# A spectral mixer and token MLP on one core: the filter rows in 20 loads of two pieces instead of 28 of three

## The chip, the cores and the metric

The kernel runs on one core of a Trainium2 chip. The metric is the device time of one execution in microseconds (us); lower is better. The core has engines that run side by side, each through its own list of instructions: TensorE (PE, matrix products; its weight loads are shown as PEld), VectorE (DVE), ScalarE (ACT), GpSimd (POOL) and SyncE (SP), which here only issues transfers. Transfers (DMA) between the device memory and the on-chip memory run on 16 DMA engines beside the compute engines. An engine goes through its list in order, and where an instruction needs what another engine or a transfer makes, it waits on a semaphore; all that stands behind it on the same engine waits too.

## What is computed

The input is a sequence of 2048 rows with 512 numbers each. It is normalised row by row, transformed by a real two-dimensional FFT, multiplied by a complex filter `w_r + 1j * w_i` of 2048 x 257 numbers, transformed back and added to the input. A second part normalises the sum, and mixes along the sequence with an MLP of 1376 hidden units:

```
h  = x + irfft2(rfft2(layernorm(x)) * (w_r + 1j * w_i))
u  = gelu(einsum("bsd,sf->bdf", layernorm(layernorm(h)), w1) + b1)
h2 = h + (einsum("bdf,fs->bds", u, w2) + b2) transposed
```

The second line's two normalisations are the one ahead of the MLP part and the one inside it. All inputs and outputs are in bf16.

## The kernel before

The transforms are matrix products with constant tables. The 2048 rows are held as 128 partitions x 16 (`NS2`), and the transforms go through these stages, named after the helper functions that emit them:

- A (line 593): the first step of the transform along the sequence, 16 groups of four matmuls, with the tables F scaled by each row's deviation into FS. Y holds the result.
- B (line 637), the transform along the 512 columns, and C (line 652), the second step along the sequence, for 16 chunks c of 8 of the 128 columns of Y. B is evicted into six buffers Bsb, C into two buffers Xsb, each for a pair of chunks.
- P (`emit_P`, line 669; the instruction is on line 674): VectorE multiplies one chunk by the filter. P of chunk c reads `W[:, 2*c:2*c+2]`, that is two of the 32 filter rows (`NTAU`) that each partition holds, both components, and writes one of six buffers P.
- I (`emit_I`, instruction on line 692): the first inverse step, eight matmuls for a chunk, which read P. Its eviction Ie (lines 708 and 709) goes to TT.
- Bi, Ai (lines 771, 801 to 808 and the variants for the first group): the remaining inverse steps, then the sum h, its normalisation HH, and the MLP: `m1` (line 844, first weights W1), the gelu, and `m2` (line 962, second weights W2), with the output added and stored.

The filter tile W has 128 partitions x 32 rows x 2 components x 256 columns in bf16, 4 MB. The filter rows lie in device memory in another order than the partitions want, and half of them are read backwards, so W can't be loaded in one transfer. The list `pieces` on line 510 cuts the 32 rows of all partitions into stretches. For each stretch, each component and each of two groups of partitions there is one load of the stretch read forward and one read backward; the stretch that starts at row 0 needs one more load for its first row. Each load writes 32 partitions in runs of 512 bytes. That gives 12 loads for the first stretch and 8 for each other.

All loads of one stretch form a group (`group=f"W{pi}"`) with one semaphore. In `gen_sync` an instruction that reads anything of a group waits for the count of the whole group:

```
v = count[d.lane] if d.is_dma else d.lane_idx
```

So a P waits until every load of the stretch that holds its two rows has landed. P0 to P3 read the stretch of rows 0 to 7, P4 to P8 that of rows 8 to 17, P9 to P15 that of rows 18 to 31.

The order of the work on each engine is fixed. `schedule` (line 249) takes written lists for the compute engines (line 979), which name nearly every operation of these stages. On VectorE the products and the evictions between them stand there as `P0 P1 Ie0_0 P3 P2 Be7 P4 Be8 P5 Ie2_0 P7 P6 Ie4_0 P9 P8 Ie6_0 P10 P11 Ie7_0 P13 P12 Ie10_0 P14 P15`. On TensorE the same stretch ends with `C10p I6 I5 B14 C12p I7 B15 I8 I9 C14 I10 C15 I11 I12 I13 I14 I15`. SP issues transfers by their `prio`: first X and F (a part of X is issued by ScalarE), then E, Lm and Hm, then the filter loads stretch by stretch, then ID, GD and IF, the eight loads of W1 and the eleven of W2. Those behind the filter loads also wait for the last eviction of stage A (`gate`, line 737). GpSimd issues three small loads, of the biases B1s and B2s.

Of the kernel before, what the change touches and what calls it, by code (L numbers as in the profile page):

```python
# [465 lines left out]
def build_kernel(nc, A_x, A_w_r, A_w_i, B_w1, B_b1, B_w2, B_b2, out, verbose=False):  # L466
# [40 lines left out]
    dma("ld_L", "sp", Lm[:], cin["L"][:, :, :, :], 2 << 16, prio=0.51)  # L507
    dma("ld_H", "sp", Hm[:], cin["H"][:, :, :, :], 1 << 17, prio=0.52)

    pieces = [(0, 8), (8, 18), (18, 32)]  # L510
    for pi, (ta, tb) in enumerate(pieces):
        for comp, wsrc in enumerate((A_w_r, A_w_i)):
            wv = wsrc.rearrange("(q r) k -> q r k", r=64)
# [515 lines left out]
def bass_sequential_preLN__spectral_gfnet__mixer_token_mlp__prompt_kernel(  # L1029
    nc,  # L1030
    A_x,
    A_w_r,
    A_w_i,
    B_x,
    B_w1,
    B_b1,
    B_w2,
    B_b2,
    out,
):  # L1040
    build_kernel(nc, A_x, A_w_r, A_w_i, B_w1, B_b1, B_w2, B_b2, out)
# [28 lines left out]
```

## Time and profile before

| what | value |
|---|---|
| median of 5 runs | 130.63 us (129.92 to 132.82) |
| the profiled execution | 130.18 us, of which the profile's span is 128.4 us |
| TensorE busy | 121.7 us, 95% of the span |
| VectorE busy, ScalarE busy | 65.1 us each, 51% |
| filter products on VectorE (line 674) | 16 of 0.68 us, from 20.2 to 36.3 us |
| filter loads issued by SP | 28, from 6.53 to 25.94 us |
| granted TensorE clock | 1.0 throughout |

The profile shows one execution. Times in it count from the start of its span. A line of a timeline gives start, duration, engine, source line, operation, what it writes and reads, and how many instructions are merged; a bracket at its end tells how long the engine had been idle before and what ended the wait. A line of a DMA view gives the tile and its source, the issuing queue, the number of issues, the size of one and the median time from issue to landing. A line of windows gives, for a stretch of time, each engine's busy time and instruction count, the granted TensorE clock, the mean busy share of the DMA engines and the rate in GB/s. Matmuls overlap, so that the durations of single ones add up to more than the time they take together.

### The profile page before, as it was taken

The page shows a single profiled execution, that of the slowest core. Times are in us where ns is not written, and L with a number is a line of the kernel's source. Part 1 is how long each engine was busy: PE and PEld are TensorE (multiplying, and loading weights), DVE is VectorE, ACT ScalarE, POOL GpSimd, SP SyncE. Part 2 cuts the span into 40 slices and gives each one's busy share as a digit, 9 for nine tenths or more (in the row PEclk, how much of TensorE's full clock was granted, in tenths as well). Part 3 has the DMA queues.
Part 4 walks back from the last instruction along what each step waited for, and adds up shares of the span by engine and source line. Part 5 has one row for each costly group of instructions (what it writes and reads, how often), then busy time and mean ns, then how long its engine had stood idle before and what let it go on. Part 6 is the DMA issues. An engine that isn't in the chain of part 4 may idle for free.

```text
span 128.4 us, 2036 instructions
## 1 busy us (share of the span) xinstructions
PE 121.7 (95%) x777; PEld 74.4 (58%) x786; DVE 65.1 (51%) x141; ACT 65.1 (51%) x137; POOL 12.6 (10%) x33
## 2 busy tenths in 40 slices
PE   6969979999999999999999999999999999999990
PEld 2337657777776655545444444456666666666660
DVE  1679948997978999967750000000423323324322
ACT  4779979999968989898777711222000000000000
POOL 0049980310000000000000000000000000000000
PEclk9999999999999999999999999999999999999999
DMA  3999899999999999999100000000111121121121
GB/s 107 339 396 371 254 209 212 300 278 357 394 422 422 420 417 417 276 361 400 59 0 0 0 0 5 0 0 0 41 67 55 41 79 49 41 82 41 41 84 41
DMA packets 16505, 22.71 MB, mean 177 GB/s; under 512 B 1552, under 2 KB 12304, under 8 KB 16368
## 3 DMA queue, kind: packets, MB, share of 16 engines
q1 hardware_dynamic: 15808, 21.66, 49.1%
q10 hardware_dynamic: 576, 0.92, 2.0%
q8 instruction: 6, 0.10, 0.3%
q0 software_dynamic: 112, 0.01, 0.2%
q14 instruction: 3, 0.02, 0.1%
HBM read 20.49 MB, written 2.10 MB: 176 GB/s over the span
## 4 chain that ended last, share of the span: by engine, by line
PE 86%; DMA 6%; SPq 2%; ACT 1%; issue 1%; DVE 1%; POOL 0%
PE ps L844 29%; PE ps L962 28%; PE ps L692 6%; DMA F<-c_F 6%; PE ps L637 6%; PE ps L771 5%; PE ps L652 3%; SPq L490 2%; PE ps L593 2%; PE ps L808 2%; PE ps L968 2%; ACT Y L607 1%; PE ps L911 1%; DVE OUT L974 1%; POOL FS L577 0%
## 5 line engine op out<-in xcount | busy, mean ns | idle before, releaser
L844 PE MATMUL ps<-HH,W 128*128 128x512 bf16 (+1 forms) x168 | 39.4, 379 | 0.2
L962 PE MATMUL ps<-GT,W 128*128 128x512 bf16 (+1 forms) x162 | 35.7, 379 | 0.2
L974 DVE SCALAR_TENSOR_TENSOR OUT<-ps,B2f,H 128x512 bf16<-128x512 f32 x16 | 12.0, 751 | 46.7 <-PE ps L962 24.4
L962 PEld LDWEIGHTS ps<-GT,W 128*128 128x128 bf16 (+1 forms) x165 | 23.7, 144 | 12.0
L844 PEld LDWEIGHTS ps<-HH,W 128*128 128x128 bf16 (+1 forms) x170 | 16.9, 100 | 17.6 <-issue 0.2
L944 ACT ACTIVATE GT<-ps,B1f 128x512 bf16<-128x512 f32 (+1 forms) x11 | 7.0, 691 | 12.7 <-PE ps L844 11.8
L818 DVE TENSOR_TENSOR H<-ps,X 128x512 bf16<-128x512 f32 x14 | 9.7, 691 | 4.0 <-PE ps L808 3.4
L824 ACT ACTIVATE SQ<-H,nm 128x512 bf16<-128x512 bf16 x14 | 10.1, 721 | 2.7 <-DVE H L818 2.4
L674 DVE TENSOR_TENSOR P<-Xsb,W 128x1024 bf16<-128x1024 bf16 x16 | 10.4, 684 | 0.9 <-DMA W<-in_A_w_i_dram 0.8
L559 DVE BATCH_NORM_STATS2 st<-X 128x6 f32<-128x512 bf16 x13 | 8.3, 679 | 3.7 <-DMA X<-in_A_x_dram 3.7
L781 ACT ACTIVATE EO<-ps 128x512 bf16<-128x512 f32 x15 | 8.8, 587 | 0.9 <-PE ps L771 0.7
L637 PE MATMUL ps<-E,Y 128*128 128x256 bf16 x64 | 8.5, 273 | 0.7 <-ACT Y L607 0.7
L593 PE MATMUL ps<-FS,X 128*128 128x256 bf16 x64 | 7.9, 273 | 1.3 <-POOL FS L577 1.2
L771 PE MATMUL ps<-GD,TT 128*128 128x256 bf16 x60 | 9.0, 272 | 0.1
L692 PE MATMUL ps<-Hm,P 128*128 128x128 bf16 x128 | 8.9, 220 | 0.0
L692 PEld LDWEIGHTS ps<-Hm,P 128*128 128x128 bf16 x128 | 7.4, 98 | 1.7 <-issue 1.3
L577 POOL TENSOR_SCALAR FS<-F,rs 128x256 bf16<-128x256 bf16 x16 | 7.4, 481 | 7.8 <-DMA F<-c_F 7.2
L533 PE MATMUL ps<-WM 128*128 128x512 bf16 (+1 forms) x19 | 7.0, 523 | 1.2 <-DVE eps L525 1.2
L665 ACT ACTIVATE Xsb<-ps 128x1024 bf16<-128x1024 f32 (+1 forms) x9 | 8.0, 884 | 0.0
L641 ACT ACTIVATE Bsb<-ps 128x512 bf16<-128x512 f32 x13 | 7.3, 594 | 1.2 <-PE ps L637 1.2
L593 PEld LDWEIGHTS ps<-FS,X 128*128 128x128 bf16 x64 | 5.4, 97 | 3.7 <-POOL FS L577 2.2
L771 PEld LDWEIGHTS ps<-GD,TT 128*128 128x128 bf16 x60 | 5.8, 98 | 3.0 <-ACT EO L781 0.2
(70 smaller groups left out, 97.2 us busy)
## 6 DMA issues: line engine op xcount, KB each, us to landing
W<-in_B_w_dram SPq DMA_DIRECT2D x8, 688.0 KB, 13.5
W<-in_B_w_dram SPq DMA_DIRECT2D x10, 512.0 KB, 18.3
out_dram<-OUT SPq DMA_DIRECT2D x16, 128.0 KB, 1.7
X<-in_A_x_dram SPq DMA_DIRECT2D x4, 256.0 KB, 6.7
F<-c_F SPq DMA_DIRECT2D x4, 256.0 KB, 7.0
IF<-c_IF SPq DMA_DIRECT2D x1, 1024.0 KB, 8.0
W<-in_A_w_r_dram SPq DMA_DIRECT2D x4, 224.0 KB, 3.8
W<-in_A_w_i_dram SPq DMA_DIRECT2D x4, 224.0 KB, 4.3
```

Of the source, the lines that this page charges most:

```text
L559: K.op(f"bn{n2}", "dve", lambda e, eng, n2=n2: eng.bn_stats(st[:, n2, 0:6], X[:, n2, :]), ins=[X[:, n2, :]], outs=[st[:, n2, 0:6]], occ=62 ...
L593: r = eng.matmul(ps[:, b, 256 * u:256 * u + 256].rearrange("p (a b) -> p a b", a=2), X[:, n2, 128 * t:128 * t + 128], fr if t < 2 else fa, ...
L637: r = eng.matmul(o, Y[:, k, c, :], E[:, k, :].rearrange("p (h r) -> p h r", h=2), start=(i == 0), stop=(i == 3), skip_group_check=True)
L674: return eng.tensor_tensor(P[:, :, :, :], x.unsqueeze(2).broadcast_to([NP, 2, 2, 256]), W[:, 2 * c:2 * c + 2, :, :], ALU.mult)
L692: r = eng.matmul(o, P[:, h, m, par::2], Hm[:, v, m, :].rearrange("p (m r) -> p m r", r=4), start=(h == 0 and m == 0 and (par == 0 or b != ...
L771: r = eng.matmul(o, TT[:, q, n2, par, :], GD[:, par, q, :], start=(i == 0), stop=(i == 3), skip_group_check=True)
L781: return eng.activation(eo[:, :], ps[:, bE, :], ACT.Copy)
L818: K.op(f"h{n2}", "dve", lambda e, eng: eng.tensor_tensor(H[:, n2, :], ps[:, bA, :], X[:, n2, :], ALU.add), ins=[ps[:, bA, :], X[:, n2, :]] ...
L824: K.op(f"sq{n2}", "act", lambda e, eng: eng.activation(sq[:, :], hsrc, ACT.Square, bias=nm[:, n2, 0:1], accum_out=s2t[:, n2, 0:1]), ins=[h ...
L844: return eng.matmul(ps[0:Mt, bank, :], W1[:, n2, 128 * t:128 * t + Mt], HH[:, n2, :], start=(n2 == 0), stop=(n2 == 15), skip_group_check=True)
L962: r = eng.matmul(ps[:, b, :], W2[t][0:Kt, n2::16], GT[0:Kt, t, :], start=(t == 0), stop=(t == NFT - 1), skip_group_check=True)
L974: K.op(f"fin{n2}", "dve", lambda e, eng, n2=n2, b=b: eng.scalar_tensor_tensor(OUT[:, n2, :], ps[:, b, :], B2f[:, n2:n2 + 1], H[:, n2, :], ...
```

## The change

The 32 rows are cut into two stretches, rows 0 to 11 and rows 12 to 31, instead of three.

```
-    pieces = [(0, 8), (8, 18), (18, 32)]
+    pieces = [(0, 12), (12, 32)]
     for pi, (ta, tb) in enumerate(pieces):
         for comp, wsrc in enumerate((A_w_r, A_w_i)):
             wv = wsrc.rearrange("(q r) k -> q r k", r=64)
```

There are 12 loads for the first stretch (four each of 192, 16 and 176 KB) and 8 of 320 KB for the second; before there were 12 (128, 16 and 112 KB), 8 of 160 KB and 8 of 224 KB. The bytes are the same. P0 to P5 now wait for the first group and P6 to P15 for the second. In VectorE's order the first product that needs the second group is P7; before, P4 and P9 were the first of their groups. The instructions of TensorE, VectorE, ScalarE and GpSimd and their order stay as they are; the list of SP is shorter by eight, and what stands behind the filter loads moves forward by that much.

More of the change, by code (lines that the diff above doesn't have):

```diff
@@ L508, in build_kernel @@
     dma("ld_H", "sp", Hm[:], cin["H"][:, :, :, :], 1 << 17, prio=0.52)
-    pieces = [(0, 8), (8, 18), (18, 32)]
+    pieces = [(0, 12), (12, 32)]
     for pi, (ta, tb) in enumerate(pieces):
```

## The prediction

> **What bounds the kernel now.** I read the page's busy table and chain first, for the engine that sets the end.
>
> ```profile
> PE 121.7 (95%) x777; PEld 74.4 (58%) x786; DVE 65.1 (51%) x141; ACT 65.1 (51%) x137; POOL 12.6 (10%) x33
> ...
> PE 86%; DMA 6%; SPq 2%; ACT 1%; issue 1%; DVE 1%; POOL 0%
> ```
>
> The reader is to see that TensorE is the bound and that its own waits are short. A filter load can move the end only through VectorE: load, product P (L674), the inverse matmuls (L692) that read P, and TensorE's place in its fixed order. So the second view is the groups, for a P that waits on a load.
>
> ```profile
> L674 DVE TENSOR_TENSOR P<-Xsb,W 128x1024 bf16<-128x1024 bf16 x16 | 10.4, 684 | 0.9 <-DMA W<-in_A_w_i_dram 0.8
> ```
>
> One wait, 0.8 us. The third view, VectorE's timeline from 23.7 to 37 us, says which P it is. In VectorE's written order the products stand P0 P1 P3 P2 P4 P5 P7 P6 P9 P8 P10 and so on, with evictions (CAST) in between.
>
> ```profile
> 24.41 0.69 DVE L674 TENSOR_TENSOR P<-Xsb,W 128x1024 bf16<-128x1024 bf16 x1
> 25.02 0.68 DVE L642 CAST Bsb<-ps 128x512 bf16<-128x512 f32 x1
> 25.62 0.68 DVE L674 TENSOR_TENSOR P<-Xsb,W 128x1024 bf16<-128x1024 bf16 x1
> 26.22 0.68 DVE L709 CAST TT<-ps 128x512 bf16<-128x512 f32 x1
> 26.82 1.28 DVE L674 TENSOR_TENSOR P<-Xsb,W 128x1024 bf16<-128x1024 bf16 x2
> 28.12 0.69 DVE L709 CAST TT<-ps 128x512 bf16<-128x512 f32 x1
> 29.62 1.29 DVE L674 TENSOR_TENSOR P<-Xsb,W 128x1024 bf16<-128x1024 bf16 x2 [0.80 <-DMA W<-in_A_w_i_dram]
> ...
> 35.03 1.28 DVE L674 TENSOR_TENSOR P<-Xsb,W 128x1024 bf16<-128x1024 bf16 x2
> ```
>
> P7 and P6 are the pair at 26.82, P9 and P8 the pair at 29.62: P9 waits for the third piece. From 29.62 VectorE runs without a break to the end of P15 at 36.31. The fourth view is the DMA issues, each of the last loads of the three pieces asked for alone (issued at 13.93, 19.20 and 25.27).
>
> ```profile
> W<-in_A_w_i_dram SPq DMA_DIRECT2D x1, 112.0 KB, 3.0
> ...
> W<-in_A_w_i_dram SPq DMA_DIRECT2D x1, 160.0 KB, 5.1
> ...
> W<-in_A_w_i_dram SPq DMA_DIRECT2D x1, 224.0 KB, 4.3
> ```
>
> So the pieces are complete at 16.9, 24.3 and 29.6 us. The first products that need them start at 20.20, 24.41 and 29.62. The last view is the TensorE timeline at the end of this stage.
>
> ```profile
> 32.30 1.06 PE L692 MATMUL ps<-Hm,P 128*128 128x128 bf16 x16
> ...
> 34.50 2.57 PE L692 MATMUL ps<-Hm,P 128*128 128x128 bf16 x40
> ```
>
> The 16 take 1.06 us. Without the last one's own 0.22 that is 15 steps of 0.056. The 40 at this step would take 39 x 0.056 + 0.22 = 2.40, and they take 2.57. The 0.16 that is left is the last group, I15, waiting for P15. This is all that TensorE loses here to a late VectorE.
>
> **The change, part by part.**
>
> Issue. The old order issues 28 filter loads from 6.53 to 25.94, 0.65 us each with their gap, and the 16 KB loads cost as much as the 224 KB ones. Eight fewer save 8 x 0.65 = 5.2 us of SP's queue. Nothing waits for SP there: X and F are issued before it and do not move, and the loads behind (ID, GD, IF, then the MLP weights) get up to 5.2 us earlier. IF lands at 27.07 + 8.0 = 35.1 and is first read at 38.6, so no wait goes. Zero on the path, hidden by TensorE's continuous work.
>
> First piece, 12 rows instead of 8. It has 12 loads as before, so its last issue stays at 13.93, but 1.57 MB instead of 1.05 MB. In the old run the first of its loads (128 KB) lands at 12.9 and the seventh at 10.67 + 3.8 = 14.5: 512 KB in 1.6 us, 330 GB/s; the whole stretch from 12 to 14.5 shows a mean of 338 GB/s. At 338 the new first load lands at 13.1 and the other 1.38 MB 4.1 us later, at 17.2. P0 reads it at 20.20. Cover 3.0 us, cost zero. P4 and P5 now wait for this piece and no longer for one that arrives 0.1 us before P4 starts.
>
> Second piece, 20 rows, 2.62 MB, first needed by P7 instead of P9. This is the step that decides. Behind P7 in VectorE's order stand P6, the eviction of I4, P9 and everything after; P6 and P7 also hold the buffer that the eviction of C10 (29.60 on ScalarE) fills. The transfer stretches of the old trace:
>
> ```profile
> 17.00:20.00 3.00, 2.89 (x29) 2.18 (x30) 1.30 (x2) 2.07 (x5) 2.14 (x4) 1.00 0.96 255
> 20.00:22.50 2.50, 2.50 (x34) 1.76 (x31) 2.20 (x5) 2.45 (x5) 0.00 (x0) 1.00 0.91 183
> ...
> 27.00:28.50 1.50, 1.50 (x22) 1.21 (x23) 1.48 (x3) 1.50 (x3) 0.58 (x2) 1.00 1.08 316
> ```
>
> ```profile
> DMA packets 6515, 3.32 MB, mean 266 GB/s; under 512 B 513, under 2 KB 6408, under 8 KB 6509
> ```
>
> The first fence has windows (last column GB/s, the one before it the DMA share), the second is the DMA view from 17 to 29.5. The arrival of the second piece, X, is 17.2 plus 2.62 MB over a rate. At 338 GB/s, the best the old trace shows for these rows, X = 25.0. At the mean of 266, dips included, X = 27.0. The upper end adds a laggard: the last load of the old second piece took 5.1 us against 3.0 for the last of the first piece, 2.1 more. If all of that comes on top of 27.0, X = 29.1. I take 27.0. The old rate was partly held down by issue (DMA share 0.96 in 17 to 20, where each 160 KB load takes 0.66 us to issue, 248 GB/s), which 320 KB per issue lifts, but the dip at 20 to 22.5, where the small B1s and B2s loads pass, stays.
>
> What X does. P9 could have started when the cast at 28.12 was over, 28.81, that is 2.0 us after P7's start. It started at 29.62. So P7 may start up to 0.8 late, at 27.62, before the later products are any later than they are now; with 0.1 from landing to start that is X = 27.5. I6 starts on TensorE at 29.43 and needs P6, X + 0.1 + 1.3: 28.9 at X = 27.5, in time. Above 27.5, P15 and with it I15 slip one for one, since VectorE has no break from P9 to P15. Below 27.5, P15 comes earlier by up to 0.4 (the evictions of I7 and C14 hold it), but TensorE can use only 0.16.
>
> At X = 27.0: P7 starts 0.3 late, P9 at 29.1 instead of 29.62, the 0.8 wait is gone, a wait of 0.3 before P7 takes its place, and I15 follows I14 directly. Sum: 0 (issue) + 0 (first piece) - 0.16 = -0.16 us. At the ends: X = 25.0 gives -0.16, X = 29.1 gives +1.6. After I15 TensorE goes on without a break to 125, so a shift is carried whole.
>
> The profiled execution took 130.18 us (span 128.4 and 1.8 outside it), the median of the five runs is 130.63. 130.18 - 0.16 = 130.02; the same step on the median is 130.5.
>
> **Two rules of the Trainium skill beside these rows.** The rows show that the rate does not rise with the load: 338 GB/s in the stretch of 16 to 128 KB loads, 316 in the best stretch of 224 KB loads. "DMA: Bandwidth & Descriptors", Bandwidth, says to batch to 1 MiB, with about 2 us fixed per DMA. Eight fewer loads in series would then be worth 16 us; the trace has all 28 landed 23.0 us after the first issue, so they overlap, and the rows' sum stands. Against the change speaks the same page under Rules for kernel authors: issue early and wait late. P7 now waits for the very last row. If the last byte came no earlier than today, at 29.6, P7 would start at 29.7 and the sum would be 29.7 - 27.6 = +2.1 us; the rows give the second piece a start without a gap and so the earlier X.
>
> **The rivals.**
> A, late landing (slower). The second piece arrives after X = 28.2 and P7 to P15 slip. For it: the dip of 183 GB/s, the 5.1 us load, and that P7 needs the piece 2.8 us before P9 needed the old third one. Against it: X = 28.2 needs a mean below 238 GB/s from 17.2 on, where the old queue, short of issues, had 266. Price at X = 28.2: 0.7, at 29.1: 1.6, so 131.3 to 132.2 us. It decides from X = 28.2.
> B, the old runs lose more at P9 than the profiled one (faster). The median lies 0.45 above the profiled run. If that is a later third piece, the new order, which ends its stream some 2.5 us earlier, takes it away too: 0.16 + 0.45 = 0.6, 130.0 us, or 129.9 if a little more. For it: P9 and P4 (0.1 us margin) are the only products on the edge. Against it: nothing says that the 0.45 lies here.
> C, the transfer is hidden anyway: X lies between 25 and 28.1 and the time stays within 0.65 us of 130.63. This contains the forecast. A change that does nothing is excluded, since VectorE's second wait on W moves from P9 to P7 in the written program.
>
> **How the numbers follow.** 0.5% of 130.63 is 0.65 us, about what a measurement of this kernel can tell from no change. Case C with the forecast has 0.58, A has 0.25 (the upper bound of X is as far from 28.2 as 27.0 is, and the laggard is one event seen once), B past 0.65 us has 0.17. Range: low 129.7, B with the spread of the single runs (lowest 129.92) a little undercut; high 131.7, A at X = 28.6. The forecast's own range is 130.1 to 131.0.
>
> **What would show it.** Right: 20 filter loads on SP's queue, the first load of W1 issued about 5 us earlier, the last filter load landed near 27.0; the P group's wait on W at the pair that stood at 26.82 and not at 29.62, under 0.7 us; P9 near 29.1; the 40 matmuls at 34.5 in about 2.41 us. Wrong: the wait before P7 above 0.8 us, a new TensorE wait before the groups of L692 from 29.4 on, or P0 later than 20.2. The prediction falls if a 320 KB load slows the stream or if a laggard engine holds the piece past 28.2.

## The result and the profile after

The changed kernel takes 131.69 us (median of 25 runs) against 130.71 us of the kernel before (44 runs, measured beside it). The ratio is 1.0071 with a 95% interval of 1.0053 to 1.0090: slower by 0.7%, where 130.5 us had been forecast. The profiled execution took 131.65 us with a span of 129.9. Here and below a few slow executions, most of them with a lowered TensorE clock, count in the medians but are left out of the ratios and their intervals.

The page of the changed kernel, its chain of waits and the groups of the filter products and of the matmuls that read them (count, then busy time and mean, then idle time before them and what ended it):

```profile
PE 74%; SPq 17%; DMA 4%; issue 2%; DVE 2%; DVEq 0%
...
L674 DVE TENSOR_TENSOR P<-Xsb,W 128x1024 bf16<-128x1024 bf16 x16 | 10.4, 683 | 2.7 <-DMA W<-in_A_w_i_dram 2.6
...
L692 PE MATMUL ps<-Hm,P 128*128 128x128 bf16 x128 | 9.1, 220 | 1.4 <-DVE P L674 1.3
```

The chain used to run through TensorE from 17 us on. Now it runs back from I6 through a product P to a filter load, and from there through SP's queue: 17% of the span are SP's issues. The chain goes back to the issue of the last load; that the issues set the pace is not shown by it. Its pieces at this place in order of time (start, length, what):

```profile
20.01 2.61 SPq L490
...
22.66 1.14 SPq L490
...
23.85 5.35 DMA W<-in_A_w_i_dram
...
29.29 1.30 DVE P L674 x2
...
30.64 1.07 PE ps L692 x16
```

Between them stand only gaps of 0.04 or 0.05 us: two held-up issues, the last filter load, P7 and P6, then I6 and I5. The wait of the products on the filter has grown from 0.8 to 2.6 us, and TensorE waits 1.3 us for a product. VectorE's timeline of the changed kernel says which one (a bracket is the idle time before and what ended it):

```profile
25.37 0.68 DVE L674 TENSOR_TENSOR P<-Xsb,W 128x1024 bf16<-128x1024 bf16 x1
25.98 0.69 DVE L709 CAST TT<-ps 128x512 bf16<-128x512 f32 x1
29.29 1.29 DVE L674 TENSOR_TENSOR P<-Xsb,W 128x1024 bf16<-128x1024 bf16 x2 [2.62 <-DMA W<-in_A_w_i_dram]
30.50 0.68 DVE L709 CAST TT<-ps 128x512 bf16<-128x512 f32 x1
31.10 1.28 DVE L674 TENSOR_TENSOR P<-Xsb,W 128x1024 bf16<-128x1024 bf16 x2
```

The pair P7 and P6, which could have begun after the cast at 25.98, begins at 29.29; P9 and P8 come at 31.10 instead of 29.62. On TensorE's timeline:

```profile
30.64 1.07 PE L692 MATMUL ps<-Hm,P 128*128 128x128 bf16 x16 [1.31 <-DVE P L674]
...
35.72 2.82 PE L692 MATMUL ps<-Hm,P 128*128 128x128 bf16 x40
```

I6 and I5 start at 30.64 (29.43 before), and the 40 matmuls at the end take 2.82 us instead of 2.57, with the last two groups waiting for their products. From the first matmul of stage B (17.11 before, 16.94 after) to the first of line 864 (37.55 and 39.03) the stage took 20.44 us and takes 22.09, 1.65 us more. From there to the end of the span both take 90.8 us. The profiled executions lie 1.47 us apart, since the stage began 0.17 earlier in the second.

SP's timeline and the DMA view of single loads (the last of each piece) show how late the filter is issued and lands:

```profile
6.65 4.00 SPq L490 DMA_DIRECT2D W<-in_A_w_r_dram  x6
10.70 4.98 SPq L490 DMA_DIRECT2D W<-in_A_w_i_dram  x6
15.71 2.67 SPq L490 DMA_DIRECT2D W<-in_A_w_r_dram  x4
18.43 6.69 SPq L490 DMA_DIRECT2D W<-in_A_w_i_dram  x4
25.16 0.78 SPq L490 DMA_DIRECT2D ID<-c_ID  x1
```

```profile
W<-in_A_w_i_dram SPq DMA_DIRECT2D x1, 176.0 KB, 3.0
...
W<-in_A_w_i_dram SPq DMA_DIRECT2D x1, 320.0 KB, 5.3
```

Single issues that took 0.6 us now take up to 2.6 (the one at 20.01). Six issues of the second row take 4.98 us instead of 3.86, and the last four take 6.69. The first piece's last load is issued at 15.07 and lands 3.0 us later, at 18.0 (forecast 17.2); the second piece's last is issued at 23.85 and lands 5.3 later, at 29.2 (forecast 27.0). Eight loads fewer brought ID, the next transfer, forward by 0.8 us, from 25.94 to 25.16, not by 5.2.

### The profile page after: what moved, and what is told of

Its sections match the earlier page's. It is cut to its first block, busy times and chain, and to the rows that moved or that the text cites. A ratio compares the mean times of both kernels' runs of the same rounds, so it can differ in the third digit from the quotient of the medians.

```text
span 129.9 us, 2027 instructions
## 1 busy us (share of the span) xinstructions
PE 121.2 (93%) x777; PEld 74.2 (57%) x786; DVE 65.0 (50%) x141; ACT 65.2 (50%) x137; POOL 12.2 (9%) x33
## 4 chain that ended last, share of the span: by engine, by line
PE 74%; SPq 17%; DMA 4%; issue 2%; DVE 2%; DVEq 0%
PE ps L844 28%; PE ps L962 27%; SPq L490 17%; PE ps L771 5%; PE ps L692 4%; DMA W<-in_A_w_i_dram 4%; PE ps L808 2%; PE ps L968 2%; PE ps L911 1%; DVE P L674 1%; PE ps L652 1%; PE ps L637 1%; DVE OUT L974 1%; PE ps L864 0%; PE ps L801 0%
## 5 line engine op out<-in xcount | busy, mean ns | idle before, releaser
L844 PEld LDWEIGHTS ps<-HH,W 128*128 128x128 bf16 (+1 forms) x170 | 16.9, 100 | 17.5 <-issue 0.2
L674 DVE TENSOR_TENSOR P<-Xsb,W 128x1024 bf16<-128x1024 bf16 x16 | 10.4, 683 | 2.7 <-DMA W<-in_A_w_i_dram 2.6
L533 PE MATMUL ps<-WM 128*128 128x512 bf16 (+1 forms) x19 | 6.1, 468 | 1.2 <-DVE eps L525 1.2
```

The source lines that it names most:

```text
L674: return eng.tensor_tensor(P[:, :, :, :], x.unsqueeze(2).broadcast_to([NP, 2, 2, 256]), W[:, 2 * c:2 * c + 2, :, :], ALU.mult)
L844: return eng.matmul(ps[0:Mt, bank, :], W1[:, n2, 128 * t:128 * t + Mt], HH[:, n2, :], start=(n2 == 0), stop=(n2 == 15), skip_group_check=True)
```

## The experiments

Two theories stood against each other. Theory W: the filter's last row arrives near 29.2 us whatever the cut, and the time depends on which product has to wait for it. Rival L: the larger loads hold SP up and so delay the rows. Beside these, theory B: the three small bias loads, which pass through the DMA engines at the same time, delay the piece.

**The grain of the wait alone.** Two kernels have the same 28 loads in the same order, with cuts at rows 12 and 22. In the first the second and third stretch share one group, so that P7 waits for all rows to 31 as in the changed kernel; in the second each stretch has its group.

```
-    pieces = [(0, 12), (12, 32)]
+    pieces = [(0, 12), (12, 22), (22, 32)]
...
-                        prio=1.0 + pi, group=f"W{pi}", wgroup=f"W{pi}")
+                        prio=1.0 + pi, group=f"W{min(pi, 1)}", wgroup=f"W{min(pi, 1)}")
```

> 28 loads again: rows 0 to 11, 12 to 21 and 22 to 31, but the second and the third stretch share one group, so that P7 waits for both as in the changed kernel. This keeps the wait of the change and takes away the larger loads. Theory W: the last filter load still lands near 29.2 to 29.5, P7 waits some 2.6 us, time as with the change, 131.5 to 131.9 us. Rival L: with loads of 160 KB SP is not held up, the stream ends near 27.5, and the time is within 0.3% of before.

Measured: 131.89 us, ratio to the kernel before 1.0088 (1.0053 to 1.0124). The last filter load landed at 30.0, and P7 waited as in the changed kernel. Its VectorE timeline:

```profile
30.09 1.29 DVE L674 TENSOR_TENSOR P<-Xsb,W 128x1024 bf16<-128x1024 bf16 x2 [3.07 <-DMA W<-in_A_w_i_dram]
```

The second kernel is the first without the change to `group` and `wgroup`.

> The loads of three12_onegroup (rows 0 to 11, 12 to 21, 22 to 31, 28 loads in the same order and sizes), now with a group of their own for the second and the third stretch. Nothing but the grain of the waits differs between the two. Theory W (the grain of the wait is the whole cost): rows 12 to 21 land near 24.6 us, P7 does not wait, rows 22 to 31 land near 30.0 and P11, the first that needs them, starts near 32, so no product waits behind P0 and the time is 130.1 to 130.6 us, 1.0% below three12_onegroup. Rival L (the arrangement of the loads costs, not the wait): 131.5 us or more.

Measured: 129.89 us, ratio 0.9950 (0.9927 to 0.9972). Its VectorE timeline:

```profile
26.77 1.28 DVE L674 TENSOR_TENSOR P<-Xsb,W 128x1024 bf16<-128x1024 bf16 x2
28.13 0.69 DVE L709 CAST TT<-ps 128x512 bf16<-128x512 f32 x1
28.74 1.28 DVE L674 TENSOR_TENSOR P<-Xsb,W 128x1024 bf16<-128x1024 bf16 x2
30.10 0.69 DVE L709 CAST TT<-ps 128x512 bf16<-128x512 f32 x1
30.71 1.28 DVE L674 TENSOR_TENSOR P<-Xsb,W 128x1024 bf16<-128x1024 bf16 x2
```

No product waits for the filter any more, although the last row lands later than ever, at 30.7. The two kernels move the same bytes in the same loads and differ by 1.4% (by their ratios to the kernel before), some 1.8 us, twice the change itself. That settles W against L for the cost. Nor did the smaller loads bring the rows earlier, as L had it: their last rows landed at 30.0 and 30.7, against 29.2 with the larger loads. It also gives a kernel that is 0.5% faster than the kernel before and 1.2% faster than the changed one.

**The cut moved.** With 20 loads in two pieces, but the cut elsewhere.

```
-    pieces = [(0, 12), (12, 32)]
+    pieces = [(0, 16), (16, 32)]
```

> Pieces of rows 0 to 15 and 16 to 31, still 20 loads in two groups. Theory W (the stream of 4.2 MB ends near 29.2 us however it is cut, and what counts is which product waits for its end): P7 is freed and P9 becomes the first product that waits. P9 starts near 29.3 as in the kernel before (29.62), the wait before P7 is gone, time as before, 130.5 to 130.9 us. The first piece grows to 2.1 MB and lands near 19.6, just ahead of P0 (20.0). Rival L (loads of 192 to 320 KB stop SP's issue and so delay the whole stream): the end of the stream stays late or gets later, and the time is still 0.3% or more above before.

Measured: 130.32 us, ratio 0.9945 (0.9905 to 0.9985). The wait before P7 went, as theory W said, and the kernel with 20 loads is no slower than the one with 28. But the two pieces landed otherwise than expected: the first at 20.8, not 19.6, and the second at 27.8, not 29.3. In the profiled execution (130.68 us) the wait has gone to P0, as VectorE's timeline shows, while the 40 last matmuls take 2.42 us without a wait among them:

```profile
20.81 1.29 DVE L674 TENSOR_TENSOR P<-Xsb,W 128x1024 bf16<-128x1024 bf16 x2 [1.04 <-DMA W<-in_A_w_i_dram]
```

The single runs spread from 129.52 us up (six of the twelve lie up to 129.97, the other six from 130.68 on), which fits a first piece that lands on the edge of P0, but which runs waited was not recorded.

```
-    pieces = [(0, 12), (12, 32)]
+    pieces = [(0, 18), (18, 32)]
```

> Two pieces, rows 0 to 17 and 18 to 31, 20 loads: the other end of the trade. The first piece is 2.36 MB, 0.26 MB more than with the cut at 16, where it landed at 20.8; at 250 GB/s it lands near 21.8, so that P0, which could start at 19.9, waits 1.8 us. TensorE has no slack there (I0 stands 0.1 us behind P0), so the stage slips by about 1.7 us; P9 no longer waits. Time 131.5 to 132.2 us. If the first piece had slack as I predicted: 130.5 us.

Measured: 131.51 us, ratio 1.0070 (1.0031 to 1.0110). The first piece landed at 20.9 and P0 waited 1.39 us, 0.4 less than expected; TensorE waited 1.22 us for it. So the first piece has an upper limit, near 16 rows, where P0 already waited in the profiled execution, and beyond it the cost comes back at the other end. The second piece landed at 27.1, although one filter load here took 2.63 us to issue, the longest of all. So the first half of theory W, an end of the stream that does not depend on the cut, does not hold (27.1 to 30.7 in these profiles), and neither does L's, that held-up issues make that end late. The second half of W, that the time depends on which product waits, stands.

```
-    pieces = [(0, 12), (12, 32)]
+    pieces = [(0, 10), (10, 32)]
```

> Pieces of rows 0 to 9 and 10 to 31, 20 loads in two groups. Theory W: the stream again ends near 29.2, but now P5, which could start at 25.4, waits for it. P5 and the eviction of I2 come to stand behind the wait, two operations of 0.6 us more than in the changed kernel, so the end slips by another 1.2 us: about 132.9 us. Rival L: 20 loads as in the changed kernel with nearly the same sizes, hence nearly the same time, 131.7 us, unless the waiter matters.

Measured: ratio 1.0113 (1.0065 to 1.0160), some 131.5 to 132.7 us. Neither forecast, 132.9 or 131.7, is told apart well: the interval takes in the second and leaves the first out by little. The profiled execution (134.29 us) had a lowered TensorE clock, 0.987, and serves only for the place of the wait: P5 starts at 29.66 after 4.34 us, with the second piece landed at 29.64.

**The bias loads.** The three loads of GpSimd are made to wait for the last eviction of the first inverse step, which puts them behind the filter.

```
-    gate = [o for o in K.ops if o.name == "Ye15"]
+    gate = [o for o in K.ops if o.name == "Ye15"]; late = [o for o in K.ops if o.name in ("Ie15_0", "Ie15_1")]
...
-    dma("ld_b1a", "pool", B1s[:, 0:10], B_b1[0:1280].rearrange("(t p) -> p t", p=NP), 2560, prio=20, after=gate)
-    dma("ld_b1b", "pool", B1s[0:96, 10:11], B_b1[1280:1376].rearrange("(t p) -> p t", p=96), 192, prio=20, after=gate)
-    dma("ld_b2", "pool", B2s[:, :], B_b2.rearrange("(p s2) -> p s2", s2=NS2), 4096, prio=20, after=gate)
+    dma("ld_b1a", "pool", B1s[:, 0:10], B_b1[0:1280].rearrange("(t p) -> p t", p=NP), 2560, prio=20, after=late)
+    dma("ld_b1b", "pool", B1s[0:96, 10:11], B_b1[1280:1376].rearrange("(t p) -> p t", p=96), 192, prio=20, after=late)
+    dma("ld_b2", "pool", B2s[:, :], B_b2.rearrange("(p s2) -> p s2", s2=NS2), 4096, prio=20, after=late)
```

> The changed kernel, with the three small bias loads of GpSimd's queue put behind the last eviction of the first inverse step (near 38 us) and so out of the filter stream. Theory B (the 2-byte rows of the bias loads hold some of the DMA engines up between 20.5 and 23 us, and the filter group waits for the slowest engine): the last filter load lands 1 to 1.7 us earlier, near 27.5 to 28.2, the wait before P7 falls from 2.6 to 1 to 1.6 us, time 130.6 to 131.0 us. If the bias loads do not matter: 131.7 us and a wait of 2.6 us as with the change.

Measured on the changed kernel: 130.44 us, ratio 0.9995 (0.9966 to 1.0024). Its window from 20 to 22.5 us, with the GB/s last, and its VectorE timeline:

```profile
20.00:22.50 2.50, 2.50 (x35) 1.74 (x34) 2.20 (x4) 2.45 (x5) 0.00 (x0) 1.00 1.12 312
```

```profile
28.39 1.29 DVE L674 TENSOR_TENSOR P<-Xsb,W 128x1024 bf16<-128x1024 bf16 x2 [1.64 <-DMA W<-in_A_w_i_dram]
```

The same window of the changed kernel reads 207 GB/s:

```profile
20.00:22.50 2.50, 2.50 (x36) 1.74 (x35) 2.28 (x4) 2.45 (x5) 0.00 (x0) 1.00 0.99 207
```

Without the bias loads the second piece lands at 28.3 instead of 29.2 and the wait before P7 falls by 1.0 us. The landing and the wait of 1.64 us are just outside the expected 27.5 to 28.2 and 1 to 1.6. A difference of 0.9 us between two single profiles is little: the same 28 loads ended at 30.0 and 30.7 in the two kernels above. The times say more: the loss of the change is gone within the interval, which lies clear of that of the changed kernel (1.0053 to 1.0090). In the profiled execution (130.79 us) the stage still took 21.11 us, 0.67 more than before. SP's held-up issues stay: the one at 20.24 still takes 2.27 us, so the bias loads don't cause that one.

> The kernel before, with only the three bias loads moved behind the first inverse step. If theory B is right, its third piece also lands about 0.9 us earlier, near 28.6, and the 0.8 us wait before P9 goes; TensorE loses no more than the 0.16 us that it waits for the last product, so 130.2 to 130.6 us, a gain of 0.1 to 0.3%. If the bias loads matter only in the changed kernel: no change in the wait before P9.

Measured on the kernel before: 130.46 us, ratio 0.9983 (0.9951 to 1.0015). This expectation failed in its mechanism. The third piece landed at 29.5 as before and P9 still waited 0.98 us:

```profile
29.62 1.29 DVE L674 TENSOR_TENSOR P<-Xsb,W 128x1024 bf16<-128x1024 bf16 x2 [0.98 <-DMA W<-in_A_w_i_dram]
```

The last load was issued at 25.38 and took 4.2 us to land, as before (25.27 and 4.3). The window from 20 to 22.5 us has 238 GB/s instead of 183, but the end of the stream did not move. Why the bias loads cost something in the changed kernel and not here was not tested.

> Both remedies together, three groups with the cut at row 12 and the bias loads late. By theory W three12 has no wait on a filter load left, so that taking the bias loads out gains nothing more: within 0.2% of three12. If it is clearly faster than three12, the filter stream costs TensorE time in another way than through the waits of VectorE.

Measured with cuts at 12 and 22, three groups and the bias loads late: 129.95 us, ratio 0.9952 (0.9926 to 0.9977), the same as with the cuts alone. Where no product waits, the bias loads cost nothing.

## Why the prediction was wrong

- What bounds the kernel, and how a filter load can reach the end: right. The loss came by the way named, from load to P7, to I6 on TensorE, to a shift carried whole to the end.
- Issue, zero on the path: right as a direct cost. The saving of 5.2 us of SP's queue did not come, 0.8 us was left, because five issues were held up by about 5 us together. The trace before had two such issues already, 1.10 us at 19.86 and 0.85 at 23.01, which the flat 0.65 us passed over.
- First piece, landing at 17.2 with 3.0 us of cover: it landed at 18.0 with 2.0 us of cover. Its last load took 3.0 us from issue to landing in both kernels, but was issued at 15.07 instead of 13.93, behind a held-up issue at 10.70. Zero was right.
- Second piece, X = 27.0 with ends at 25.0 and 29.1: this is the step that failed. X was 29.2, a little outside the upper end. I took the mean rate of 266 GB/s of the old stretch and argued that the old queue had been short of issues, so that larger loads would make it no slower. 2.62 MB from 18.0 to 29.2 is 235 GB/s, below the 238 from which the prediction let rival A decide. Of the 2.2 us, 0.8 come from the later start and 1.3 from the rate.
- Within that step, about half of the 1.3 was a misreading. The 266 counts all traffic from 17 to 29.5 us, 3.32 MB, and the loads behind the filter were issued from 25.94 on. The old second and third pieces are 3.15 MB, and they came between 16.9, when the first piece was complete, and 29.5: 250 GB/s. That would have given X = 27.7 from the forecast start, already beyond the threshold of 27.5, and 28.5 from the real one. The other half is a stream slower than the old one, 235 against 250. In the run with the bias loads moved the second piece, from 18.5 to 28.3, has 267 GB/s, so that some 0.9 us of the landing goes with them there. Why they delay this piece and not the old third one stays open.
- The threshold, X = 27.5 and one for one above it: right. 29.2 - 27.5 = 1.7, and the stage became 1.65 us longer. Three profiles where P7 waits give the same line. Counted from the first matmul of stage B, the last filter load landed 11.28 us (bias loads moved), 12.26 us (the change) and 12.70 us (cuts at 12 and 22, one group) later, and the stage took 0.67, 1.65 and 2.10 us more than before: each time what goes beyond 10.6 us. The threshold of 27.5 is 10.4 on this count, 0.2 too early. The place of the new wait, the pair P7 and P6, was right, its 0.3 us was not.
- The gain of 0.16 us once no product waits: right for the profiled execution. From the first matmul of stage B to line 864 it is 20.30 us with the cuts at 12 and 22 against 20.44, 0.14 less, and the 40 last matmuls take 2.43 us.
- Rival A, 131.3 to 132.2 us, is what happened: 131.69. Rival B may be right in what it said of the kernel before. Where the waits on the filter are gone, the gain is 0.5%, 0.65 us, four times what the profiled execution shows, so other executions of the kernel before presumably lose more there; they were not profiled, and it is not shown. The change replaced that wait by a larger one.
- The rule for early issue and late waiting (the Trainium skill, "DMA: Bandwidth & Descriptors", Rules for kernel authors) was weighed with +2.1 us if the last byte came at 29.6. It came at 29.2 and the stage lost 1.65. The rule for large loads on the same page speaks for the change. Between 28 loads and 20 the last filter row's landing moved from 29.5 to 29.2 in these profiles, and the batching gained nothing; no filter load of any run is larger than 352 KB, so the rule's 1 MiB was not tried. The 2 us per transfer that the prediction set beside it stand on that page under the path of transfers issued from GpSimd, not under Bandwidth; the filter loads are issued by SP.

The cause of the loss is shown: the coarse wait, by the two kernels that differ in it alone. What holds the issues up is not shown. The held-up times grow with the loads: in the first piece the longest issue took 0.72 us with 128 KB loads, 0.75 with 160 KB (cut at row 10), 1.54 with 192 KB (12), 2.01 with 256 KB (16) and 2.63 with 288 KB (18). With 320 KB loads each of the four late issues ended at about the time at which only three earlier loads were left to land. A limit on what may wait in the DMA queues would look like this; it was not tested by itself.

## What to carry to other kernels

When loads are merged into larger groups, look at the first consumer in the written order of the group that grows, and ask when the group's last byte lands, not the first row that it wants: here P7 took over a deadline 2.8 us earlier than P9's. Price that landing by those loads' own bytes over the time in which they landed (250 GB/s here), not by all that a window moved (266), and don't count on a gain in pace from a queue that seems short of issues. A cut belongs where the consumer behind it has slack: the same 28 loads cost 1.4% more or less by the semaphore alone, and two pieces cut at row 16 did as well as three.

## What the runs showed of the hardware

- A transfer's issue on SP, 0.6 us otherwise, took up to 2.6 us, and with 320 KB loads it ended when about three earlier loads had not yet landed. Fewer and larger loads therefore did not free SP's queue by their number: eight fewer saved 0.8 us of it.
- Two of the bias loads, 6.5 KB together in rows of 2 and 32 bytes, were under way beside the filter. In the window from 20 to 22.5 us the changed kernel had 207 GB/s with them and 312 without, the kernel before 183 and 238, the cuts at 12 and 22 with three groups 150 and 199. With these two and the third of 0.2 KB moved away, the 2.6 MB piece of the changed kernel was complete 0.9 us earlier; the third piece of the kernel before was not.
